# Attention with a relative bias, then a snake feed-forward layer, on one core: the loads of the prologue put in another order

## The chip, the cores and the metric

The kernel runs on one core of one Trainium2 chip. The metric is the device time of one execution in microseconds (us); every kernel is run several times, and the median is compared. The engines are named as in the profile: PE is TensorE, DVE is VectorE, ACT is ScalarE, POOL is GpSimd, and SP is SyncE, which here only issues DMAs. ACT and POOL issue DMAs too, each into a queue of its own.

## The reference

Two layers follow each other. The first is attention over 8 batches of 8 heads, with 576 positions of 64 elements, and a bias that depends only on the distance between two positions. The second takes the result as 4608 rows of 512 and is a feed-forward layer with a periodic activation.

```python
# attention: q, k, v are [8, 8, 576, 64], bias_table is [32, 8]
scores = scale * np.matmul(q, k.transpose(0, 1, 3, 2))
n = np.abs(pos[:, None] - pos[None, :])
bucket = np.where(n < 16, n, large)        # large: logarithmic in n, at most 31
scores = scores + bias_table[bucket].transpose(2, 0, 1)[None]
attn = softmax(scores)
x = (attn @ v).transpose(0, 2, 1, 3).reshape(4608, 512)
# feed-forward: w_in is [512, 2048], w_out is [2048, 512], alpha is [2048]
h = x @ w_in
g = h + np.sin(alpha * h) ** 2 / (alpha + 1e-9)
out = g @ w_out
```

Inputs and output are float32. The kernel works in float16 with float32 sums.

## The kernel before

**Steady work.** The kernel goes through the batches t = 0 to 7. For each it works on four pairs of heads. For a pair, PE multiplies q and k into PSUM (`sc`), ACT takes the exponential into a tile `u` (line 594; two such tiles take turns), DVE multiplies a band of `u` by a table of exponentiated biases (lines 606 and 623, tables `mhr` and `m2r`), and PE multiplies `u` by v (`av`). The last 64 of the 576 key positions don't fill a block of 128, so their v rows of two heads share a tile of their own, `vh`, beside the main tile `v`; every `av` product begins with the `vh` matmul. DVE divides by the row sums, PE turns the result round, and it is put into `xT`. After a batch's attention comes one block of 512 rows of the second layer: 16 steps f = 0 to 15, in each of which PE multiplies `xT` by `w_in` (four matmuls), ACT takes the sine (line 715), one of ACT, DVE and POOL squares it (lines 722 and 724; POOL only in block 0), and DVE forms g (line 729). The products of g with `w_out` (`mo`) are put between other work of PE, mostly into the next batch's attention.

**Prologue.** For batches 0 and 1, q and k come in by plain loads (tiles `natx`, `nat`) and PE turns them round (lines 495 and 501); from batch 2 on they are staged in DRAM by POOL's DMAs (`stage_kq`, line 330) and loaded with a transposing DMA. v of batches 0 and 1 is loaded as float32 into a staging area that lies inside the tile of `w_out` (`vst`, `vhst`), and POOL casts it into `v` and `vh` (`cast_v`, lines 367 and 369). The loads of `w_out` must therefore come behind the casts of v of batch 1. POOL also loads `w_in` and clears the second set of key tiles (`clear`, lines 391 to 399).

The bias table is made on the chip: a matmul with a constant `phi` gives a row of 512 values a head (`e_sb`, 8 partitions); ACT writes it to DRAM (`e_dram`), and `m2r` and `mhr` are read back from there with one element of offset per partition. POOL loads `m2r` of the first two heads, SP loads `mhr` and the rest of `m2r`. alpha is loaded by SP behind these, turned round on PE (line 541), and 1/alpha is made from it.

**Order.** Each engine runs its instructions in the order in which they are emitted. The prologue's order is written out by hand in the kernel's body (lines 429 to 472). All that follows is ordered by a planner (`Plan`): it knows a cost for each task and engine and times before which a task can't start (`T_M2` and `T_MH` for the bias tables, `T_V` for v, `T_TR1` for k and q of batch 1, `T_W` and `T_WO` for the weights; the second number is for the later pairs, q, or batch 1), and at each step it emits the task that can start first. These times are constants in the source; the chip waits on semaphores whatever they say. The planner counts POOL as free from its start time on; the prologue's work on POOL is not in it. The staging of batch 2 is emitted with the first matmul of batch 0, so on POOL it stands directly behind the prologue.

Of the kernel before, what the change touches and what calls it, by code (L numbers as in the profile page):

```python
# [10 lines left out]
F16 = mybir.dt.float16  # L11
F32 = mybir.dt.float32
# [38 lines left out]
class Cell:  # L51
    v = None
# [105 lines left out]
OFFSET = 8  # L158
T_START = 7.0
T_PAIR = ((7.0, 8.5), (10.5, 13.0), (10.5, 13.0))  # L160
T_M2 = (16.7, 20.5)
T_MH = (18.5, 20.5)
T_V = (17.7, 47.5)
T_TR1 = (37.5, 41.5)
T_W = 31.0
T_WO = 58.0
WARM0 = 6
WARM1 = 1
AV_PRI = 250
# [18 lines left out]
def kernel(  # L188
# [39 lines left out]
    for x in range(EW - 1):  # L228
# [18 lines left out]
    w_out16 = sgl.tile([128, NF, DM], F16, name="w_out16")  # L247

    wv = w_out16.rearrange("p f n -> p (f n)")
    vst = wv[:, 0 : 2 * 4 * H * D].bitcast(F32).rearrange("p (c h d) -> p c h d", c=4, h=H)  # L250
    vhst = wv[:, 2 * 4 * H * D : 2 * 4 * H * D + 2 * NP * D].bitcast(F32).rearrange(
        "p (hp d) -> p hp d", hp=NP
    )
# [103 lines left out]
    def load_v32(t, eng):  # L357
        vp = v[t].rearrange("h s d -> s h d")
        for c in range(4):
            eng.dma_start(out=vst[:, c], in_=vp[128 * c : 128 * c + 128])  # L360
        vq = v[t].rearrange("(hp two) s d -> two s hp d", two=2)
        for z in range(2):
            eng.dma_start(out=vhst[64 * z : 64 * z + 64], in_=vq[z, 512:S])  # L363

    def cast_v(t, engs):
        for c in range(4):
            engs[c].tensor_copy(out=vs[t][:, c, :, 0:D], in_=vst[:, c])
        for z in range(2):
            engs[4 + z].tensor_copy(  # L369
                out=vhs[t][64 * z : 64 * z + 64, :, VC * z : VC * z + D],  # L370
                in_=vhst[64 * z : 64 * z + 64],
            )

    def load_nat(dst, h0, h1, src, eng):

        eng.dma_start(out=dst, in_=src[h0:h1].rearrange("h (p i) d -> p h (i d)", i=SI))  # L376
# [32 lines left out]
    def cast0(kq, eng):  # L409
        eng.tensor_copy(  # L410
            out=natb[:, kq], in_=nat0[:, kq].rearrange("s two (i d) -> s i two d", i=SI)
        )

    def load_m2r(eng, h0, h1):

        eng.dma_start(
            out=m2r[:, h0:h1],
            in_=bass.AP(tensor=e_dram, offset=EW * h0, ap=[[1, 128], [EW, h1 - h0], [1, XW]]),
        )

    def load_mhr(eng):
        for z in range(2):
            eng.dma_start(
                out=mhr[64 * z : 64 * z + 64],
                in_=bass.AP(tensor=e_dram, offset=EW * z + 192,
                            ap=[[1, 64], [2 * EW, NP], [1, 192]]),
            )

    load_nat(nat0[:, 0], 0, 2, k[0], nc.sync)
    load_nat(nat0[:, 1], 0, 2, q[0], nc.sync)  # L430
    nc.scalar.dma_start(out=tabN, in_=bias_table)
    nc.scalar.dma_start(
        out=tabL,
        in_=bass.AP(tensor=bias_table.tensor, offset=bias_table.offset + (NB - 1) * H,
                    ap=[[0, NB], [1, H]]),
    )
    nc.scalar.dma_start(out=phi_sb, in_=phi_h.ap())
    nc.sync.dma_start(out=id_sb, in_=idm.ap())
    nc.scalar.preload_act_table_set(EXP_SET)
    for kq, src in ((0, k), (1, q)):  # L440
        load_nat(nat1[:, kq, 0:2], 2, 4, src[0], nc.gpsimd)
    load_v32(0, nc.sync)
    for kq, src in ((0, k), (1, q)):
        load_nat(nat1[:, kq, 2:6], 4, H, src[0], nc.gpsimd)

    nc.vector.memset(zz, 0.0)
    clear(nc.vector, 0)
# [5 lines left out]
    warm(WARM1)  # L453
    nc.scalar.activation(out=e_sb, in_=eps_[0:H, 0:EW], func=AF.Copy)
    nc.scalar.dma_start(out=e_dram.ap(), in_=e_sb)
    cast0(0, nc.vector)
    cast0(1, nc.gpsimd)
    load_m2r(nc.gpsimd, 0, 2)
    load_mhr(nc.sync)
    load_m2r(nc.sync, 2, H)  # L460
    nc.sync.dma_start(out=alphaN, in_=moe_alpha.rearrange("(f p) -> f p", p=128))
    nc.sync.dma_start(out=idf_sb, in_=idf.ap())
    P_ = nc.gpsimd
    load_w_in16((0,))
# [21 lines left out]
    def plan_tr(t, p, kq, pri, nb, deps=()):  # L486

        b, c = Buf("mo"), Cell()

        def mm(e):  # L490
            c.v = new_mo().bitcast(F16)
            for i in range(SI):
                x = i * SN
                if t == 0 and p == 0:
                    nc.tensor.transpose(
                        out=c.v[:, x : x + SN], in_=natb[:, kq, i], identity=id_sb[0:SN, 0:SN]
                    )
                    continue
                for z in range(2):
                    h = 2 * p - 2 + z if t == 0 else 2 * p + z  # L500
                    nc.tensor.transpose(
                        out=c.v[64 * z : 64 * z + 64, x : x + SN],
                        in_=(nat1 if t == 0 else nat2)[:, kq, h, D * i : D * i + D],
                        identity=id_sb[0:SN, 0:SN],
                    )

        def cp(e):
            pin = c.v[:, 0:S].rearrange("d (i p) -> d p i", i=SI)

# [24 lines left out]
        return [x], [plan.add({"DVE": 0.25}, tail, [x], pri + 30)]  # L534
# [322 lines left out]
```

## Time and profile before

| | |
|---|---|
| median of 6 runs | 423.59 us (421.27 to 425.47) |
| the profiled execution's own time | 423.19 us |
| its span in the profile | 421.4 us |
| granted PE clock, mean | 0.975 |
| busy: PE, ACT, DVE, POOL | 398.5, 335.8, 292.1, 89.2 us |
| DMA moved | 41.90 MB, 99 GB/s over the span |

The profile is of one execution. In its lists, a row has the start in us, the duration in us, the engine, the line of the kernel, the operation with what it writes and reads, and in brackets how long the engine was idle before and what ended that. A "q" behind an engine's name (SPq, POOLq) is its sequencer, which issues DMAs. A table of stretches has, for each, the busy time and the number of instructions of PE, weight loads, DVE, ACT and POOL, then the granted PE clock as a share of full speed, the busy share of the DMA engines and the GB/s that they moved. The chain is followed back from the last instruction, at each step to what released it.

The tile names in the trace are those of the memory: v's staging area appears as `w_out`, so `w_out<-in_v_dram` is a load of v and `w_out<-in_moe_w_out_dram` one of the weights.

### The profile page before, as it was taken

Reading aid. Unit: us, or ns where it says so; the run is one execution under the profiler, and the core shown is the slowest. Engines: PE = TensorE matmul, PEld = TensorE weight load, DVE = VectorE, ACT = ScalarE, POOL = GpSimd, SP = SyncE. Lnnn points to the kernel's source line nnn. Section 1 sums busy time; section 2 is a strip of 40 time slices with the busy share of each in tenths; the row PEclk is TensorE's granted clock in tenths of the full one; section 3 lists DMA queues with packets and bytes.
Section 4 is the critical chain, followed back from the end, with each engine's and each line's share of the span. In section 5 each row is a group of like instructions: output and inputs, shape, how many; then the busy total and the mean of one; then the engine's idle time right before and its main releaser. Section 6 shows DMA issues by size and latency. Waiting matters only on the chain.

```text
span 421.4 us, 8752 instructions
## 1 busy us (share of the span) xinstructions
PE 398.5 (95%) x3518; PEld 230.2 (55%) x3518; DVE 292.1 (69%) x683; ACT 335.8 (80%) x497; POOL 89.2 (21%) x100
## 2 busy tenths in 40 slices
PE   6786778999999999999999999999999999999996
PEld 2465334775467545764576456644775466544442
DVE  5868568675966695769666967687667867799300
ACT  4747648887988899879987998889888988899411
POOL 3376837206200350017000800040000000000000
PEclk8869979999999999999999999999999999999999
DMA  9989599998990399029920992095000010000111
GB/s 179 199 173 220 87 186 166 148 133 98 149 173 27 98 153 169 27 62 155 175 56 32 161 179 75 26 151 131 27 26 26 0 51 26 26 2 0 51 75 75
DMA packets 136232, 41.90 MB, mean 99 GB/s; under 512 B 121720, under 2 KB 130736, under 8 KB 136192
## 3 DMA queue, kind: packets, MB, share of 16 engines
q0 software_dynamic: 89632, 18.26, 52.1%
q1 hardware_dynamic: 46400, 23.05, 24.5%
q8 instruction: 27, 0.44, 0.4%
q14 instruction: 13, 0.11, 0.1%
q10 hardware_dynamic: 160, 0.04, 0.0%
HBM read 37.76 MB, written 16.52 MB: 129 GB/s over the span
## 4 chain that ended last, share of the span: by engine, by line
PE 85%; DMA 7%; POOL 4%; SPq 2%; DVE 1%; ACT 0%; issue 0%; POOLq 0%; ACTq 0%
PE sc L402 44%; PE mo L402 29%; PE av L402 10%; DMA w_out<-in_v_dram 6%; PE av L676 2%; SPq L360 1%; SPq L363 1%; DVE g L729 1%; POOL w_out L386 1%; POOL w_out L360 1%; DMA tabN<-in_bias_table_dram 1%; POOL staged_k L330 1%; POOL staged_q L330 1%; POOL w_in L381 0%; POOL nat L376 0%; ACT s L715 0%
## 5 line engine op out<-in xcount | busy, mean ns | idle before, releaser
L594 ACT ACTIVATE u<-sc 128x768 f16<-128x768 f32 (+1 forms) x224 | 165.7, 789 | 33.9 <-PE sc L402 29.6
L402 PE MATMUL mo<-w_out,g 128*128 128x512 f16 x576 | 156.3, 379 | 0.0
L402 PE MATMUL sc<-xT,w_in 128*128 128x512 f16 x576 | 132.9, 383 | 5.5 <-DVE g L729 5.5
L729 DVE SCALAR_TENSOR_TENSOR g<-sq,inv_a,sc 128x512 f16<-128x512 f16 x144 | 104.7, 747 | 13.5 <-ACT sq L722 6.1
L715 ACT ACTIVATE s<-sc,alphaT 128x512 f16<-128x512 f32 x144 | 92.3, 678 | 16.5 <-PE sc L402 15.7
L402 PEld LDWEIGHTS <-w_in 128*128 128x128 f16 x576 | 55.9, 98 | 71.6 <-issue 8.7
L402 PE MATMUL sc<-qT,kz 128*128 128x192 f16 (+1 forms) x512 | 90.8, 292 | 4.0 <-DVE g L729 1.5
L623 DVE TENSOR_TENSOR u<-u,m2r 128x512 f16<-128x512 f16 (+1 forms) x192 | 70.5, 388 | 20.0 <-ACT u L594 17.5
L402 PEld LDWEIGHTS <-g 128*128 128x128 f16 x576 | 55.7, 98 | 45.2
L402 PEld LDWEIGHTS <-u 128*128 128x128 f16 x1440 | 56.1, 98 | 12.6 <-issue 3.2
L402 PEld LDWEIGHTS <-kz 128*128 128x128 f16 x512 | 43.8, 99 | 24.7 <-issue 7.1
L348 POOL DMA_DIRECT2D v<-in_v_dram x24 | 21.3, 901 | 161.9 <-PE av L402 161.9
L402 PE MATMUL av<-v,u 128*128 128x65 f16 x1280 | 55.5, 195 | 0.0
L722 ACT ACTIVATE sq<-s 128x512 f16<-128x512 f16 x73 | 46.0, 630 | 2.3
L402 PE MATMUL av<-vh,u 128*128 128x130 f16 x160 | 35.5, 222 | 3.0 <-POOL vh L369 3.0
L665 DVE RECIPROCAL rd<-av 128x6 f32<-128x6 f32 x64 | 12.0, 187 | 37.2 <-PE av L402 37.2
L666 DVE TENSOR_TENSOR xn<-av,rd 128x384 f16<-128x384 f32 x64 | 31.4, 491 | 2.2
L724 DVE TENSOR_TENSOR sq<-s 128x512 f16<-128x512 f16 x66 | 28.4, 431 | 3.5 <-ACT s L715 2.9
L484 DVE COPY outs<-mo 128x512 f32<-128x512 f32 x27 | 18.6, 690 | 10.0 <-PE mo L402 9.9
L676 PEld LDWEIGHTS <-xn 128*128 128x128 f16 x160 | 13.9, 99 | 17.1 <-DVE xn L666 5.4
L482 ACT ACTIVATE outs<-mo 128x512 f32<-128x512 f32 x9 | 5.4, 597 | 22.4 <-PE mo L402 22.4
L676 PE MATMUL av<-id_sb,xn 128*128 128x128 f16 x160 | 19.5, 222 | 3.0 <-DVE xn L666 3.0
(66 smaller groups left out, 189.4 us busy)
## 6 DMA issues: line engine op xcount, KB each, us to landing
out_dram<-outs SPq DMA_DIRECT2D x36, 256.0 KB, 2.0
staged_k<-in_k_dram POOLq DMA_DIRECT2D x6, 576.0 KB, 11.7
staged_q<-in_q_dram POOLq DMA_DIRECT2D x6, 576.0 KB, 17.4
kz<-kraw SPq DMA_DIRECT2D x12, 288.0 KB, 6.8
v<-in_v_dram POOLq DMA_DIRECT2D x24, 128.0 KB, 5.8
w_in<-in_moe_w_in_dram POOLq DMA_DIRECT2D x4, 512.0 KB, 7.9
w_out<-in_moe_w_out_dram POOLq DMA_DIRECT2D x4, 512.0 KB, 9.3
w_out<-in_v_dram SPq DMA_DIRECT2D x4, 256.0 KB, 9.5
```

The costliest lines, as they stand in the source:

```text
L348: nc.gpsimd.dma_start(out=vs[t % 2][:, c, :, 0:D], in_=vp[128 * c : 128 * c + 128],)
L402: nc.tensor.matmul(out=out, lhsT=lhsT, rhs=rhs, start=start, stop=stop)
L484: k_of(e).tensor_copy(out=o, in_=i)
L594: nc.scalar.activation(out=o, in_=x, func=AF.Exp, scale=0.125)
L623: nc.vector.tensor_tensor(out=io, in0=io, in1=m2[:, 2 * p : 2 * p + 2, x0 : x0 + hi - lo], op=ALU.mult,)
L665: nc.vector.reciprocal(out=r, in_=a[:, :, :, D])
L666: nc.vector.tensor_tensor(out=xn.v[:, 0:nq].rearrange("p c (z d) -> p c z d", z=2), in0=a[:, :, :, 0:D], in1=r.unsqueeze(3).to_broadcast([ ...
L676: nc.tensor.transpose(out=tr.v[:, qc - q0 : qc - q0 + 128], in_=xn.v[:, i], identity=id_sb)
L715: nc.scalar.activation(out=s16.v, in_=h.v, func=AF.Sin, scale=alphaT[:, f : f + 1])
L722: nc.scalar.activation(out=sq.v, in_=s16.v, func=AF.Square)
L724: k_of(e).tensor_tensor(out=sq.v, in0=s16.v, in1=s16.v, op=ALU.mult)
L729: nc.vector.scalar_tensor_tensor(out=gcell[b].v[:, f, :], in0=sq.v, scalar=inv_a[:, f : f + 1], in1=h.v, op0=ALU.mult, op1=ALU.add,)
```

## The change

It has four parts. First, the table pieces of the first two heads (`m2r` of heads 0 and 1, `mhr` of pair 0) are copied on SP from `e_sb` in SBUF and no longer read from `e_dram`; for that the last main piece of v of batch 0 and its two `vh` pieces go behind them on SP, and the pieces of the other heads are loaded by POOL. Second, alpha and its identity matrix are loaded by ACT at the start, and `phi` goes first there. Third, v of batch 1 is staged in a tile of its own (`v1st`), so that the four `w_out` loads are issued directly behind its loads, ahead of its casts, and the clearing of the second key tiles moves on POOL to before the table loads. Fourth, the planner's times change, and one of its costs.

```diff
-T_M2 = (16.7, 20.5)
-T_MH = (18.5, 20.5)
-T_V = (17.7, 47.5)
-T_TR1 = (37.5, 41.5)
-T_W = 31.0
-T_WO = 58.0
+T_M2 = (12.0, 17.0)
+T_MH = (12.5, 17.0)
+T_V = (18.0, 45.0)
+T_TR1 = (33.5, 37.5)
+T_W = 30.0
+T_WO = 54.0
...
+    v1st = sgl.tile([128, 2 * (4 * H + NP) * D], F16, name="v1st")
+    vst, vhst = [], []
+    for x in (wv, v1st):
...
+    def near(eng):
+        for h in range(2):
+            eng.dma_start(
+                out=m2r[:, h],
+                in_=bass.AP(tensor=e_sb.tensor, offset=e_sb.offset + EW * h,
+                            ap=[[EW, 1], [1, 128], [1, XW]]),
+            )
+        for h in range(2):
+            eng.dma_start(
+                out=mhr[64 * h : 64 * h + 64, 0],
+                in_=bass.AP(tensor=e_sb.tensor, offset=e_sb.offset + EW * h + 192,
+                            ap=[[EW, 1], [1, 64], [1, 192]]),
+            )
...
     def load_mhr(eng):
         for z in range(2):
             eng.dma_start(
-                out=mhr[64 * z : 64 * z + 64],
-                in_=bass.AP(tensor=e_dram, offset=EW * z + 192,
-                            ap=[[1, 64], [2 * EW, NP], [1, 192]]),
+                out=mhr[64 * z : 64 * z + 64, 1:NP],
+                in_=bass.AP(tensor=e_dram, offset=EW * (z + 2) + 192,
+                            ap=[[1, 64], [2 * EW, NP - 1], [1, 192]]),
             )
...
+    nc.scalar.dma_start(out=phi_sb, in_=phi_h.ap())
     nc.scalar.dma_start(out=tabN, in_=bias_table)
     nc.scalar.dma_start(out=tabL, ...)
-    nc.scalar.dma_start(out=phi_sb, in_=phi_h.ap())
+    nc.scalar.dma_start(out=alphaN, in_=moe_alpha.rearrange("(f p) -> f p", p=128))
+    nc.scalar.dma_start(out=idf_sb, in_=idf.ap())
     nc.sync.dma_start(out=id_sb, in_=idm.ap())
...
-    load_v32(0, nc.sync)
+    vp = v[0].rearrange("h s d -> s h d")
+    for c in range(3):
+        nc.sync.dma_start(out=vst[0][:, c], in_=vp[128 * c : 128 * c + 128])
...
     nc.scalar.dma_start(out=e_dram.ap(), in_=e_sb)
+    near(nc.sync)
+    nc.sync.dma_start(out=vst[0][:, 3], in_=vp[384:512])
+    vq = v[0].rearrange("(hp two) s d -> two s hp d", two=2)
+    for z in range(2):
+        nc.sync.dma_start(out=vhst[0][64 * z : 64 * z + 64], in_=vq[z, 512:S])
     cast0(0, nc.vector)
-    cast0(1, nc.gpsimd)
-    load_m2r(nc.gpsimd, 0, 2)
-    load_mhr(nc.sync)
-    load_m2r(nc.sync, 2, H)
-    nc.sync.dma_start(out=alphaN, in_=moe_alpha.rearrange("(f p) -> f p", p=128))
-    nc.sync.dma_start(out=idf_sb, in_=idf.ap())
-    P_ = nc.gpsimd
+    cast0(1, P_)
+    clear(P_, 1)
+    load_mhr(P_)
+    load_m2r(P_, 2, H)
     load_w_in16((0,))
-    cast_v(0, (P_, P_, P_, P_, P_, P_))
+    cast_v(0, P_, range(6))
     load_w_in16((1, 2, 3))
     for kq, src in ((0, k), (1, q)):
-        load_nat(nat2[:, kq], 0, H, src[1], nc.gpsimd)
-    load_v32(1, nc.gpsimd)
-    clear(nc.gpsimd, 1)
-    cast_v(1, (P_, P_, P_, P_, P_, P_))
+        load_nat(nat2[:, kq], 0, H, src[1], P_)
+    load_v32(1, P_)
     load_w_out16()
+    cast_v(1, P_, range(6))
...
-        m = plan.add({"PE": 0.4 if t == 0 and p == 0 else 0.7}, mm, deps, pri, nb, new=[b])
+        m = plan.add({"PE": 0.4 if t == 0 and p == 0 else 0.5}, mm, deps, pri, nb, new=[b])
```

More of the change, by code (lines that the diff above doesn't have):

```diff
@@ L249 @@
     wv = w_out16.rearrange("p f n -> p (f n)")
[L250 to L253, printed above, removed]
+    v1st = sgl.tile([128, 2 * (4 * H + NP) * D], F16, name="v1st")
+    vst, vhst = [], []
+    for x in (wv, v1st):
+        n4 = 2 * 4 * H * D
+        vst.append(x[:, 0:n4].bitcast(F32).rearrange("p (c h d) -> p c h d", c=4, h=H))
+        vhst.append(
+            x[:, n4 : n4 + 2 * NP * D].bitcast(F32).rearrange("p (hp d) -> p hp d", hp=NP)
+        )
     zz = sgl.tile([128, 512], F16, name="zz")
@@ L359, in load_v32, with cast_v @@
         for c in range(4):
-            eng.dma_start(out=vst[:, c], in_=vp[128 * c : 128 * c + 128])
+            eng.dma_start(out=vst[t][:, c], in_=vp[128 * c : 128 * c + 128])
         vq = v[t].rearrange("(hp two) s d -> two s hp d", two=2)
         for z in range(2):
[L363 to L369, printed above, removed]
+            eng.dma_start(out=vhst[t][64 * z : 64 * z + 64], in_=vq[z, 512:S])
+    def cast_v(t, eng, cs):
+        for c in cs:
+            if c < 4:
+                eng.tensor_copy(out=vs[t][:, c, :, 0:D], in_=vst[t][:, c])
+                continue
+            z = c - 4
+            eng.tensor_copy(
                 out=vhs[t][64 * z : 64 * z + 64, :, VC * z : VC * z + D],
-                in_=vhst[64 * z : 64 * z + 64],
+                in_=vhst[t][64 * z : 64 * z + 64],
             )
@@ L412, in cast0 @@
         )
+    def near(eng):
[10 more added lines that the diff above has]
+                            ap=[[EW, 1], [1, 64], [1, 192]]),
+            )
     def load_m2r(eng, h0, h1):
@@ L423, in load_mhr @@
             eng.dma_start(
-                out=mhr[64 * z : 64 * z + 64],
-                in_=bass.AP(tensor=e_dram, offset=EW * z + 192,
-                            ap=[[1, 64], [2 * EW, NP], [1, 192]]),
+                out=mhr[64 * z : 64 * z + 64, 1:NP],
+                in_=bass.AP(tensor=e_dram, offset=EW * (z + 2) + 192,
+                            ap=[[1, 64], [2 * EW, NP - 1], [1, 192]]),
             )
+    P_ = nc.gpsimd
     load_nat(nat0[:, 0], 0, 2, k[0], nc.sync)
     load_nat(nat0[:, 1], 0, 2, q[0], nc.sync)
+    nc.scalar.dma_start(out=phi_sb, in_=phi_h.ap())
     nc.scalar.dma_start(out=tabN, in_=bias_table)
@@ L440 @@
     for kq, src in ((0, k), (1, q)):
-        load_nat(nat1[:, kq, 0:2], 2, 4, src[0], nc.gpsimd)
-    load_v32(0, nc.sync)
+        load_nat(nat1[:, kq, 0:2], 2, 4, src[0], P_)
+    vp = v[0].rearrange("h s d -> s h d")
+    for c in range(3):
+        nc.sync.dma_start(out=vst[0][:, c], in_=vp[128 * c : 128 * c + 128])
     for kq, src in ((0, k), (1, q)):
-        load_nat(nat1[:, kq, 2:6], 4, H, src[0], nc.gpsimd)
+        load_nat(nat1[:, kq, 2:6], 4, H, src[0], P_)
     nc.vector.memset(zz, 0.0)
```

## The prediction

> **What bounds the kernel now.** I read the page first. PE is busy 398.5 of 421.4 us, and section 2 shows where the other 22.9 us are: in the first seven slices and in the last.
>
> ```profile
> PE 398.5 (95%) x3518; PEld 230.2 (55%) x3518; DVE 292.1 (69%) x683; ACT 335.8 (80%) x497; POOL 89.2 (21%) x100
> PE   6786778999999999999999999999999999999996
> DMA  9989599998990399029920992095000010000111
> ```
>
> The table by stretches of 5 us puts 18.9 us of PE's idle time before 75 us; from 80 to 187 us PE is busy in every microsecond (20.00, 43.00 and 44.00 us of as many). The work behind the prologue is thus a fixed block on a full engine: whatever the prologue gives or takes, the end gives or takes. Next, the chain that ended last, for 0 to 60 us alone:
>
> ```profile
> 0.74 2.59 DMA tabN<-in_bias_table_dram
> 3.33 0.04 issue
> 3.37 2.77 SPq L360
> ...
> 12.83 8.93 DMA w_out<-in_v_dram
> ...
> 21.89 0.40 POOL vh L369
> ...
> 22.35 1.59 POOL w_in L381 x3
> 23.95 1.57 POOL nat L376 x2
> 25.51 2.60 POOL w_out L360 x3
> 28.12 16.13 DMA w_out<-in_v_dram
> ...
> 45.72 2.94 POOL w_out L386 x4
> 48.66 2.23 POOL staged_k L330
> 50.89 2.23 POOL staged_q L330
> ...
> 53.25 1.04 POOL sq L724
> ...
> 54.32 0.76 DVE g L729
> ...
> 55.12 5.03 PE sc L402 x14
> ```
>
> The chain is not PE's, it is POOL's queue. The tail rows of v of batch 0 (called vh0 here) land at 21.76; POOL casts them, issues w_in, k and q of batch 1 and v of batch 1 (28.12), whose last big piece lands at 44.25; it casts these, then issues four w_out loads (2.94), staged_k and staged_q of batch 2, and only then squares the sine that block 0 of the second half has wanted since 47.7 (end of the third sine in the timeline). DVE waits 4.64 us for that square, PE 4.71. The windows show what follows: PE empty from 52 to 54, and a granted clock of 0.5 until after 58.
>
> ```profile
> 52.00:54.00 2.00, 0.00 (x0) 0.00 (x0) 0.00 (x0) 0.00 (x0) 1.87 (x2) 0.51 1.19 195
> 54.00:56.00 2.00, 0.88 (x3) 0.32 (x3) 1.68 (x3) 0.00 (x0) 1.07 (x2) 0.50 1.24 206
> 56.00:58.00 2.00, 2.00 (x6) 0.67 (x5) 1.30 (x3) 0.69 (x1) 0.25 (x1) 0.50 1.24 206
> ```
>
> So the change is priced at one point: when POOL reaches that first square.
>
> **w_out ahead of the casts of v of batch 1.** This takes 2.94 us of issue from between the last cast (ends 45.7) and staged_k. The issues move to behind 34.2, where POOL has time: it spends 34.24 to 40.33 on the memsets of clear(1), which move away, and the first cast began at 40.70. They don't go out at once. POOL's DMAs show a rotation of eight: the two vh issues of batch 1, the 16th and 17th on the queue, waited 1.49 and 2.40 us for w_in loads, the 8th and 9th. With two more POOL DMAs in front (three table loads for one), the four w_out loads follow the landings of k of batch 1 (23.92 + 12.4 = 36.3), of q (24.70 + 15.0 = 39.7) and of the first two v pieces (by 40.7 and 41.9, when their casts began). The last is out at 41.9 + 0.8 = 42.7; six casts behind it (4 x 0.62 + 2 x 0.43 = 3.3) end at 46.0, against 45.7 before. Net 2.94 - 0.3 = 2.6 us earlier. That w_out itself lands earlier than 47.88 + 12.0 = 59.9 brings nothing: its first matmul ran at 69.3. The tile of its own for v of batch 1 adds no instruction; v of batch 0 stays under w_out, and its casts are done 14 us before the first w_out issue.
>
> **clear(1) moved to 6.4 us.** POOL waited 5.45 us there for e_dram (until 11.88); the memsets take 6.1 (34.24 to 40.33), so the cover falls short by 0.65. A DVE instruction of 16 columns lasted 1.75 us and ended at 36.28, beside a POOL memset that ended at 36.30; in the new place the kt copy at 8.46 can be held the same way until 10.6, but DVE was idle from 8.84 to 10.30. Cost 0 to 0.3 on DVE; the 0.65 goes into the next part.
>
> **POOL's new table loads.** Two far mhr loads and the far m2r load stand where one m2r load stood: about 0.65 + 0.65 (the vh issues' row) + 0.72, against 0.72. w_in's first load thus goes at 12.59 + 0.65 + 1.3 = 14.5, the casts of v of batch 0 run from 15.1 to 17.6. Hidden as long as vh0 lands later than that (18.8 and 21.8 before).
>
> **When vh0 lands** is the one large unknown, since the chain hangs on it one for one (each POOL step behind it is issue time or a full DMA queue: 9 tenths busy from 25 to 42). Later: (a) the near tables, 2 x 96 + 2 x 24 = 240 KB, go out on SP in front of the last v piece and vh0. At the stage's 179 to 199 GB/s that is 1.3 us; at the slowest row for such a table (m2r, 192 KB, 5.8 us from issue to landing) it is 7.3. (b) The SP and ACT queues show the same rotation of eight: the third v load, ninth of the two queues together, started at 3.37, just behind the landing of tabN, the first. With alpha and identf in front, already the first v load is ninth and waits for the first landings (k of batch 0 at 0.74 + 3.4 = 4.1) where it went at 2.17. DMA is 9 tenths busy with other loads then, so 0 to 2.0, I take 0. (c) The far tables, 720 KB, came behind vh0 on SP and now go beside it on POOL: 0 to 720/190 = 3.8. Earlier: (d) 192 KB of m2r leave POOL: 1.0. (e) w_in's first 512 KB are issued 1.9 us later and behind the far tables; vh0's two 64 KB loads took 9.7 and 8.9 us beside it, so up to about 3.5 can come back. I let (c) and (e) cancel, and (a) at the stage's rate and (d) nearly do: 0, with ends of -3.5 and +7.
>
> SP waits in front of the near tables until e_sb is there (6.69); behind it in line are the last v piece and vh0. Their issue was held anyway (the last v piece until 9.05, vh0 until 12.79), so this wait costs 0.
>
> [...]
>
> **Gone covers.** The near tables land some 3 to 9 us earlier (DVE waited 2.88 for mhr at 22.66), but the first av matmul waited for vh0's cast at 22.29, not for a table: nothing. With pair 1's tables there by then, too, the attention of batch 0 may end 0 to 4 us earlier than 43.8. That only lengthens the wait for POOL's square: nothing. **alpha** on ACT: its transpose at 26.45 waited for no DMA; its 2.67 + 0.57 us of issue leave SP, where nothing is queued behind them until 63.6; on ACT the phi load gets out 0.93 earlier, the table set goes in 0.9 later and still ends before the exp, which follows DVE's memsets at 5.1 as before: 0.
>
> **The planner's new times** and the 0.5 for 0.7 reorder the prologue. I can't read the order from a profile; one step of the second half (four matmuls, 0.86 us) done before or behind the stall is the unit: plus or minus 1.
>
> **Sum.** The square at 53.25 - 2.6 = 50.65, PE again at 52.5 instead of 55.1, the profiled execution 423.19 - 2.6 = 420.6. The median of the runs is 0.4 above the profiled one: 421.0. The stall shrinks from 4.7 to 2.1 us unless the attention ends earlier. Of the half-clock time behind it (55.1 to about 58.6) up to 1.75 us could then come back; I take none, since the clock was already down (0.63 from 20 to 25) behind the idle stretch of 3.02 us that ended at 22.34, and an earlier attention lengthens this one. [...]
>
> **Rivals.** (1) vh0 comes 2 to 3.5 us earlier, because w_in no longer crosses it: 421.0 less 2 to 3.5, 417.5 to 419. For: 64 KB took over 9 us. Against: 720 KB of far tables take w_in's place. (2) It comes 1 to 4 us later and eats the gain: 422 to 425. For: 240 + 720 - 192 = 768 KB more can be ahead of it. (3) Slower: the near tables, read out of one partition each, hold the SP queue; vh0 comes 7.3 - 1.0 = 6.3 later, 421.0 + 6.3 = 427.3. It decides from the point where vh0 lands 2.6 us later, at 24.4; SP's issue of vh0 would then lie behind 15 us. (4) The change doesn't do what it says: w_out does not load right behind v, as the rotation holds its issues to 36 to 42 us. True in part, but the gain comes from the place in POOL's line, not from the bytes: only if the rotation held the fourth issue beyond 44 would it cost, 1 us or so.
>
> **Numbers.** Measurement of this kernel can tell about 0.5%, 2.1 us, from no change. Forecast case (vh0 within 1.5 us of before, 419.5 to 422.5): 0.40. Rival 1: 0.13. Rival 2: 0.25. Rival 3: 0.20. Rival 4: 0.02. Faster by over 0.5% (below 421.5): 0.33 of the first and all of rival 1: 0.46. Slower (above 425.7): rival 3 and a tail of rival 2: 0.24. The rest, 0.30, is no change. Range: from 416.5 (rival 1 and the planner's 1 us) to 427.5 (rival 3 at the row's price).
>
> **What would show it.** Right: staged_k on POOL directly behind the vh casts, at about 46; the first square near 50.7; DVE's wait for it near 2 us, or longer with an earlier start of the second half; no wait for mhr near 22. Wrong: vh0's cast behind 24.4, SP's near issues lasting microseconds, or v of batch 1 landing later than 46. A PE wait for something else between 50 and 75 us would break the step from the stall to the end.

## The result, and the profile after

The changed kernel takes 427.17 us (median of 18 runs, 424.38 to 431.54); the kernel before, run beside it, 423.03 (39 runs). The ratio is 1.0088, with a 95% interval of 1.0064 to 1.0112: slower, by some 3.7 us by the ratio. The profiled execution took 425.41 us, before it was 423.19. The ratios here and below are of undisturbed executions alone (experiments 3 and 7 leave out four runs each, experiment 4 eight of twelve) and need not be the quotients of the medians beside them.

The page of the changed kernel, with the same three lines as were shown of before:

```profile
PE 399.5 (94%) x3518; PEld 230.3 (54%) x3518; DVE 292.3 (69%) x684; ACT 335.4 (79%) x495; POOL 91.8 (22%) x103
PE   5559799999999999999999999999999999999996
DMA  9869999999990299119930997095100010000111
```

The difference still lies in the first seven slices of PE, but it has moved to the front: the first three fell from 6, 7 and 8 to 5 each, the fourth, sixth and seventh rose to 9. The chain of the changed kernel, from 12 us on, says why (start, duration, engine or transfer, line):

```profile
12.95 1.25 SPq L428
14.25 4.46 SPq L428
18.75 9.79 DMA w_out<-in_v_dram
28.60 0.69 POOL v L372
...
30.54 2.55 PE av L408 x45
...
53.08 5.49 PE sc L408 x17
```

It goes through SP's queue. L428 is the copying of `mhr` from `e_sb`; the last main piece of v of batch 0 gets out behind it at 18.75 and lands at 28.54, vh0 at 29.54 (before: 21.76). The casts end at 30.5, the first av matmul follows at once. But after that the chain goes to and fro between PE and DVE, up to the second half, which starts at 53.08: POOL's square isn't on it any more. SP's part of the timeline, and the table by stretches (busy time of PE, weight loads, DVE, ACT, POOL, then clock, DMA share, GB/s):

```profile
8.47 4.44 SPq L422 DMA_DIRECT2D m2r<-e_sb  x2
12.95 5.75 SPq L428 DMA_DIRECT2D mhr<-e_sb  x2
18.75 1.57 SPq L482 DMA_DIRECT2D w_out<-in_v_dram  x1
20.36 4.31 SPq L485 DMA_DIRECT2D w_out<-in_v_dram  x2
```

```profile
15.00:20.00 5.00, 2.13 (x21) 1.54 (x20) 0.00 (x0) 2.30 (x4) 2.99 (x5) 1.00 0.75 28
20.00:25.00 5.00, 1.16 (x14) 0.54 (x14) 2.19 (x5) 0.30 (x1) 0.00 (x0) 1.00 0.90 214
```

From 15 to 20 us the DMA engines were busy for 0.75 of the time and moved 28 GB/s. Before, the same stretch was:

```profile
15.00:20.00 5.00, 3.48 (x39) 1.85 (x37) 4.65 (x10) 4.89 (x7) 1.08 (x2) 1.00 1.04 190
```

The packets in the changed kernel's trace are those of the near tables: from 14 to 20 us 32 to 37 of 768 bytes start in each microsecond, about 360 ns long, 26 KB/us in all (rates here count 1000 bytes as a KB; by 1024 it is 25.4). Those of the two `m2r` pieces ran from 12.9 to 20.7. POOL had issued the far tables from 13.60 to 15.7, and the first of their packets ran at 19.9: what is slow also stands in front of the others. `m2r` of the first two heads landed at 17.64 and 21.44 (before: 17.66), `mhr` of pair 0 at 23.27 and 25.69.

Who waited for that, in the timelines of DVE, PE and POOL (in brackets the idle time ahead and what ended it):

```profile
21.56 1.43 DVE L649 TENSOR_TENSOR u<-u,m2r 128x512 f16<-128x512 f16 x4 [7.62 <-DMA m2r<-e_sb]
23.02 0.76 DVE L510 COPY qT<-mo 128x576 f16<-128x576 f16 x1
23.84 0.82 PE L408 MATMUL sc<-qT,kz 128*128 128x384 f16 x2 [6.71 <-DVE qT L510]
53.90 2.20 POOL L334 DMA_DIRECT2D staged_k<-in_k_dram  x1
58.46 1.31 POOL L750 TENSOR_TENSOR sq<-s 128x512 f16<-128x512 f16 x1
```

DVE stood 7.62 us at the first multiply by `m2r`. Behind it in line was the copy of q of pair 1 (23.02), which needs no table at all, and PE stood 6.71 us for that copy. POOL came to staged_k at 53.90 and to its first square at 58.46, 5.2 us later than before (53.25); but no one waited for it, since the attention of batch 0 was as late. So the end moved by 2.2 us in this execution (421.4 to 423.6 of span) and not by 5.2: PE's idle time grew from 22.9 to 24.1, its busy time from 398.5 to 399.5.

The clock column says 1.00 up to 50 us here, and it can't be taken at its word. The same group of two `sc` matmuls took 0.82 us at 23.84 and 0.49 at 34.35, and a group of eight `av` 0.65 at 30.60 and 0.40 at 34.73 (0.65 is also what it took before, at 22.95, where the clock's record gave 0.50). In this trace the record begins only at 32.55; until then PE ran at the pace of a granted 0.5, and so the means of the clock (0.975 before, 0.996 after) aren't compared below:

```profile
30.60 0.65 PE L408 MATMUL av<-v,u 128*128 128x65 f16 x8
34.73 0.40 PE L408 MATMUL av<-v,u 128*128 128x65 f16 x8
```

### The profile page after: what moved, and what is told of

Same layout as the page of the kernel before. It is cut to its first block, busy times and chain, and to the rows that moved or that the text cites. A ratio compares the mean times of both kernels' runs of the same rounds, so it can differ in the third digit from the quotient of the medians.

```text
span 423.6 us, 8757 instructions
## 1 busy us (share of the span) xinstructions
PE 399.5 (94%) x3518; PEld 230.3 (54%) x3518; DVE 292.3 (69%) x684; ACT 335.4 (79%) x495; POOL 91.8 (22%) x103
## 4 chain that ended last, share of the span: by engine, by line
PE 87%; DVE 5%; DMA 3%; SPq 2%; ACT 1%; POOL 0%; issue 0%; ACTq 0%; DVEq 0%
PE sc L408 44%; PE mo L408 29%; PE av L408 11%; DMA w_out<-in_v_dram 2%; PE av L702 2%; SPq L428 1%; DMA tabL<-in_bias_table_dram 1%; DVE g L755 1%; DVE xn L692 1%; DVE kz L510 1%; DVE u L649 1%; DVE kt L556 1%; DVE qT L510 1%; ACT u L620 1%; DVE natx L416 0%
## 5 line engine op out<-in xcount | busy, mean ns | idle before, releaser
L620 ACT ACTIVATE u<-sc 128x768 f16<-128x768 f32 (+1 forms) x224 | 166.2, 789 | 39.9 <-PE sc L408 34.1
L691 DVE RECIPROCAL rd<-av 128x6 f32<-128x6 f32 x64 | 12.0, 188 | 37.7 <-PE av L408 37.7
L750 DVE TENSOR_TENSOR sq<-s 128x512 f16<-128x512 f16 x65 | 28.3, 435 | 5.1 <-ACT s L741 4.7
L702 PE MATMUL av<-id_sb,xn 128*128 128x128 f16 x160 | 19.4, 219 | 1.6 <-DVE xn L692 1.4
## 6 DMA issues: line engine op xcount, KB each, us to landing
staged_q<-in_q_dram POOLq DMA_DIRECT2D x6, 576.0 KB, 17.7
```

Of the source, the lines that this page charges most:

```text
L620: nc.scalar.activation(out=o, in_=x, func=AF.Exp, scale=0.125)
L691: nc.vector.reciprocal(out=r, in_=a[:, :, :, D])
L702: nc.tensor.transpose(out=tr.v[:, qc - q0 : qc - q0 + 128], in_=xn.v[:, i], identity=id_sb)
L750: k_of(e).tensor_tensor(out=sq.v, in0=s16.v, in1=s16.v, op=ALU.mult)
```

## Experiments

The theory from this profile: the near copies, each out of one partition, run at some 26 KB/us and hold SP's queue and the DMA engines (the prediction's third rival). Rivals: their place ahead of vh0 alone does it; or parts that were priced at nothing cost something.

**1. The same tables from DRAM, at the same place on SP** (e1_near_dram: the change with)

```diff
-    ap=[[EW, 1], [1, 128], [1, XW]]   # source e_sb
+    ap=[[1, 128], [1, XW]]            # source e_dram; mhr alike
```

> The changed kernel with one edit: the four near table loads read from e_dram and no longer from e_sb; place, sizes and queue stay. Theory (one source partition): in the changed kernel they moved 25 KB/us from 13.5 to 21.4 us and held every DMA queue; from DRAM rows of the same size should move at 200 KB/us, vh0 lands at 19 to 22 instead of 29.5, v of batch 1 at 42 to 45 instead of 53.0, staged_k goes out at 43 to 46, and the time is 418 to 421.5, 2 to 5 us under the kernel before. Rival (place on SP): four loads and their wait in front of the last v piece and vh0 delay these whatever they read; vh0 lands at 27 to 30 and the time stays at 425 to 428.

424.79 us, ratio 1.0048 [1.0014, 1.0082]. The near tables landed between 16.7 and 18.3, as fast as the theory says; vh0 still landed at 27.13, where the theory had 19 to 22 and the rival 27 to 30, and staged_k came at 51.76. By the ratios a little under half of the loss went (the two intervals overlap; experiment 6 has a like result), so both are partly right: the slow source, and the place. vh0 was issued at 16.49 and 17.21, 4 to 5 us earlier than in the change; its packets then ran beside POOL's far tables and w_in's first piece, which landed at 24.86.

**2. The near copies alone** (e2_near_only, on the kernel before)

```diff
     nc.scalar.dma_start(out=e_dram.ap(), in_=e_sb)
+    near(nc.sync); <last v piece, vh0>      # mhr of pairs 1 to 3 and the far m2r stay on SP
-    load_m2r(nc.gpsimd, 0, 2)
```

> The kernel before with the near tables alone: read from e_sb on SP in front of the last v piece and vh0; w_out, alpha, the clearing and the planner's times as before. Theory (one source partition): vh0 lands 7 to 9 us later than 21.8; the chain through POOL still has the four w_out issues in it, so the first square on POOL comes 7 to 8 us later than 53.3 and the time is 428 to 431. Rival (the planner's new times or the other moves did the harm): vh0 within 3 us of before and the time 423 to 425.

426.53 us, 1.0067 [1.0037, 1.0096]. The part alone costs 2.8 us. The price by vh0 missed: it landed at 24.70, 2.9 later and not 7 to 9. w_in's first piece had landed at 15.89, before vh0 was issued, and POOL issued no load from 6.94 to 25.47, so nothing competed. Here POOL's line was last, as the prediction has it:

```profile
57.06 1.03 POOL L744 TENSOR_TENSOR sq<-s 128x512 f16<-128x512 f16 x1
58.93 7.31 PE L402 MATMUL sc<-xT,w_in 128*128 128x512 f16 x24 [7.19 <-DVE g L749]
```

**3. w_out alone** (e3_wout_only, on the kernel before, with `v1st`)

```diff
     clear(nc.gpsimd, 1)
+    load_w_out16()
     cast_v(1, (P_, P_, P_, P_, P_, P_))
-    load_w_out16()
```

> The kernel before with only v of batch 1 in a tile of its own and the four w_out loads issued behind the clearing and ahead of its casts. The prediction's step: the first square on POOL 2.6 us earlier (50.7), PE's stall in block 0 2.1 us instead of 4.7, time 420 to 421.5 (2.6 less, 0.6%). Rival: POOL's line is not what binds, or w_out's bytes get in the way of v of batch 1: within 1 us of before.

422.59 us, 0.9946 [0.9912, 0.9979]: 2.3 us gained by the ratio, where the prediction had 2.6. The traced execution (423.73, no faster than before) doesn't show the step, though. vh0 landed at 16.13 and staged_k came at 44.28, but PE waited for alpha's identity matrix, which landed at 33.42 behind the far `m2r`, and then the square waited for its sine and not the reverse:

```profile
33.55 0.26 PE L545 MATMUL mo<-idf_sb,alphaN 16*128 16x16 f32 x1 [7.27 <-DMA idf_sb<-identf]
55.10 1.03 POOL L728 TENSOR_TENSOR sq<-s 128x512 f16<-128x512 f16 x1 [6.39 <-ACT s L719]
```

**4. Before without POOL's squares** (e4_no_pool_sq)

```diff
-            if b == 0:
-                engs["POOL"] = 1.2
```

> The kernel before with POOL taken from the engines that may square the sine in block 0; DVE and ACT take all. If the chain through POOL's line is what the prologue costs, the 4.7 us stall of PE and the half-clock stretch behind it go: 3 to 6 us less, 417.5 to 420.5, less some 1 us of added work on DVE and ACT (five squares of 0.4 to 0.6). If attention of batch 0 or the w_out load binds right behind, under 1 us less.

Its runs took from 416.6 to 429.2 us, with a gap from 418.4 to 422.8; the median is 424.65, the ratio 0.9881 [0.9832, 0.993]. In the traced execution (423.79) PE's longest wait in block 0 is 2.08 us and no longer 4.71, and the time is no shorter. So whether the square was the bound of before stays open.

**5. Everything but the near copies, and the near copies behind vh0** (e5_all_but_near, e6_near_behind)

```diff
 # e5: tables and v of batch 0 as before
-    near(nc.sync)                  # and the last v piece, vh0 behind it
-    load_mhr(P_); load_m2r(P_, 2, H)
+    load_m2r(P_, 0, 2); load_mhr(nc.sync); load_m2r(nc.sync, 2, H)
 # e6
-    near(nc.sync); <last v piece, vh0>
+    <last v piece, vh0>; near(nc.sync)
```

> The changed kernel with its tables and the tail of v of batch 0 as before: vh0 ahead of every table on SP, m2r of the first two heads on POOL from DRAM, mhr and the rest of m2r on SP. The own tile for v of batch 1, w_out ahead of the casts, clear at 6 us, alpha at the start on ACT and the planner's new times stay. Theory (the copies out of e_sb and what had to go behind them are the whole loss): vh0 lands near 22 again, staged_k starts near 46, time near 421, the forecast. Rival (the parts that were priced at nothing, alpha in front of tabL, clear beside DVE's cast, the planner's times, cost 1 to 2 us of their own): vh0 near 22 to 23, first qk product near 9.5 to 10 instead of 8, time 423 to 424.5, above the kernel that moves w_out alone (422.6).

430.82 us, 1.0166 [1.0116, 1.0216]: slower than the change itself, though vh0 landed at 16.04 and staged_k came at 45.12, both earlier than forecast. This fells the idea that all hangs on POOL's chain. Two waits of this kernel (total, times, longest), DVE's row and POOL's row:

```profile
DVE u L629 <- DMA m2r<-e_dram: 14.0, 2, 9.3
PE av L682 <- DVE xn L672: 12.8, 3, 8.2
33.37 1.23 DVE L629 TENSOR_TENSOR u<-u,m2r 128x512 f16<-128x512 f16 x3 [9.34 <-DMA m2r<-e_dram]
45.12 2.20 POOL L334 DMA_DIRECT2D staged_k<-in_k_dram  x1
```

The far `m2r`, issued by SP at 14.42, landed at 33.28 (before: 24.12). With vh0 there at 16, POOL issues w_in, k, q and v of batch 1 from 17.7 on, and SP's load starves beside them. Before, POOL stood until 21.8 waiting for vh0; that wait was what let the far tables through. Kernels e3, e8, e11 and e12 show the same pair: vh0 at 15.9 to 17.5, far `m2r` at 32.2 to 33.7. In e4 and e7 both lie between: vh0 at 19.4 and 19.1, far `m2r` at 27.0 and 26.9. None of these six is as slow as e5. The late table costs most with the new times, which put its multiply early: moving it to POOL ahead of w_in gives 8.7 us there (e5 to e14, by the medians) and 1.6 with the old times (e8 to e10).

> The changed kernel with the four copies out of e_sb issued behind the last main piece and vh0 on SP. Theory (the copies hold whatever is queued behind them, and the DMA engines that serve them, while they run at about 25 KB a microsecond): vh0 lands before 18, its casts wait for POOL's table loads and w_in instead; the near tables land 3 to 8 us later than in the change (m2r near 24, mhr near 27), so PE waits for the bias of pair 0 until 25 to 27; the chain through POOL is free of vh0, staged_k at 47 to 49, time 423 to 425. Rival (only the order on SP counts, the copies themselves harm nothing but what is behind them): time near 421.

428.1 us, 1.0102 [1.0047, 1.0157]: missed. vh0 landed at 15.98, as the theory had it, and staged_k came at 49.86, a little behind its 47 to 49, but the near tables, last in line, landed at 19.2 to 28.3, and the attention itself was late:

```profile
24.25 1.43 DVE L649 TENSOR_TENSOR u<-u,m2r 128x512 f16<-128x512 f16 x4 [9.83 <-DMA m2r<-e_sb]
```

So the copies cost wherever they stand: in front they delay vh0, behind they delay themselves.

**6. The source spread over four partitions** (e13_near_spread)

```diff
     nc.scalar.activation(out=e_sb[0:H], in_=eps_[0:H, 0:EW], func=AF.Copy)
+    for r in range(1, 4):          # rows of heads 0 and 1, shifted by 32 r
+        nc.scalar.activation(out=e_sb[32 * r : 32 * r + 2, 0 : EW - 32 * r],
+                             in_=eps_[0:2, 32 * r : EW], func=AF.Copy)
-    ap=[[EW, 1], [1, 128], [1, XW]]
+    ap=[[32 * EW, 4], [1, 32], [1, XW]]
```

> The changed kernel with the rows that the near copies read laid out on four partitions 32 apart: ACT copies the rows of heads 0 and 1 three more times from PSUM, shifted by 32, 64 and 96 elements, so that row p of a table is read from partition 32*(p/32). Issue places and bytes stay as in the change; ACT has three more copies (its e_sb copy's row, some 0.5 us each). Theory (the source's partitions set the rate): the 240 KB need 2.4 us at four times the 25.4 KB a microsecond of the change, or 4.9 us at twice; m2r near has landed by 17 to 18, vh0 by 22 to 25, staged_k at 48 to 50, time 422 to 425. Rival (the rate goes by the size and the kind of packet, 768 B from SBUF to SBUF, not by the partitions): near again at 21 to 26, time 427. [...]

425.95 us, 1.0051 [1.0027, 1.0075]. (`mhr`'s 64 rows lie on two of the four partitions.) Size and kind of packet are the same, the rate is not: in the fastest microsecond, 14 to 15 us, 63 KB/us of near packets against 26, and POOL's far tables flow from 14 on; the `m2r` pieces took 4.6 us (13.0 to 17.6) and not 7.8. The same stretch of the table by stretches shows it:

```profile
15.00:20.00 5.00, 2.84 (x23) 1.65 (x21) 1.60 (x5) 3.25 (x5) 2.69 (x5) 1.00 0.87 200
```

The one partition was the brake. Yet vh0 landed at 26.90: it is issued on SP behind the copies, at 18.41 and 22.54 (the issue at 18.41 alone lasts 4.1 us; why, the trace doesn't show), and its packets meet 720 KB of far tables and w_in's first piece on POOL's queue, which landed at 25.00. Taking the brake away gives 1.6 us of the 3.7; its place and what is around it keep the rest.

**7. The planner's times and the small parts alone** (each on the kernel before)

```diff
 # e7_times_only: the six T_ constants of the change, and
-    {"PE": 0.4 if t == 0 and p == 0 else 0.7}
+    {"PE": 0.4 if t == 0 and p == 0 else 0.5}
 # e11_alpha_act: ACT issues phi, tabN, tabL, alphaN, idf_sb in this order
-    nc.sync.dma_start(out=alphaN, ...); nc.sync.dma_start(out=idf_sb, ...)
 # e12_clear_early
     cast0(1, nc.gpsimd)
+    clear(nc.gpsimd, 1)
```

> The kernel before with the change's planner times and its cost of 0.5, and nothing else. Forecast of the prediction: within 1 us of before, either way (422 to 424). Rival (the earlier times pull work of the second half and of batch 1 in front of work that could have run, and cost the place on PE): 425 to 427, with a PE wait in the first 75 us that before doesn't have.

> The kernel before with phi first on ACT and alpha and its identity matrix behind tabL on ACT, and nothing else. The prediction's price: 0. Theory (tabL becomes third instead of second, lands 1.0 to 1.5 us later, and the chain over e_sb to the tables starts that much later; against it, alpha no longer queues behind the far tables): tabL lands at 5.5 to 6.5, e_sb at 7.7 to 8.2, no PE wait for alpha; 422.5 to 425. Rival (alpha at the start is a gain, as late alpha costs PE up to 7 us in single executions): 421 to 422.

> The kernel before with the memsets of clear(1) moved to about 6 us, in front of the near m2r load on POOL, and nothing else. The prediction's price: 0.65 on POOL's table load, 0 to 0.3 on DVE. Theory (DVE's SBUF-to-SBUF copies wait for the end of POOL's memset, as the cast of 0.60 us that took 1.63 in the changed kernel): DVE's first cast and kt copies lose 1 to 2 us in all between 6 and 13 us, time 0 to 1.5 us above before, 423 to 424.5. Rival (free): 422.5 to 423.5, or below, since DVE's copies beside 34 to 40 us become faster.

Times: 426.09 us, 1.0037 [1.0002, 1.0072], 1.6 us slower by the ratio, as the rival had it; in its profile DVE waits 5.22 us for `m2r` and PE 4.5 for the copy of q queued behind. alpha: 1.0 [0.9981, 1.0019]. tabL landed at 6.32, and `e_sb` was written out 1.4 later than before (8.10 against 6.71), with nothing to show for it in the time. clear: 1.0013 [0.9989, 1.0038]; no difference. In these two traces vh0 landed some 5.5 us earlier than before (15.86 and 16.28), and the time is the same. PE stood elsewhere, in the clear kernel 6.44 us for alpha, and the first square waited for its sine (3.23 and 4.38 us). So an earlier vh0 alone, the prediction's first rival, gains nothing here.

**8. The old times in the changed kernel** (e9_after_old_times)

> The changed kernel with the planner times and the cost of before (m2r from 16.7 instead of 12.0, and so on). Theory (the new times put pair 0's bias multiply on DVE ahead of the next pairs' copies, and PE pays for it while m2r is late): DVE copies q and k of pair 1 before it multiplies by m2r, PE's wait of 6.7 us for qT shrinks to under 2; 424.5 to 426. Rival (POOL's first square at 58 us binds as soon as the attention is earlier, so the gain turns into a wait for it): PE gets the work done earlier, but DVE then waits 3 to 5 us for POOL's square and the time stays at 426.5 to 428.

428.38 us, 1.0128 [1.0103, 1.0152]: the theory missed, the rival's time was nearer, though DVE has no long wait for POOL's square. In this kernel the new times are the better ones, by 0.4%. With the copies of pairs 1 and 2 ahead of the multiply, PE has that work done early and then stands in one piece until vh0's cast. The second half starts earlier, too, and there two DVE copies are held beside POOL's staging. Rows of PE, DVE and PE:

```profile
30.12 0.27 PE L408 MATMUL av<-vh,u 128*128 128x130 f16 x1 [8.40 <-POOL vh L375]
53.94 4.30 DVE L556 COPY kt<-kz 64x64 f16<-64x64 f16 x2
59.07 1.86 PE L408 MATMUL sc<-xT,w_in 128*128 128x512 f16 x4 [3.97 <-DVE g L755]
```

With vh0 late, another order only moves the stalls. What the times are worth shows where the loads are in order, as in the next kernels.

**9. Towards a kernel whose loads are in order** 

```diff
 # e8_wout_alpha: e3, and on SP behind vh0
+    alphaN, idf_sb
     load_mhr(nc.sync); load_m2r(nc.sync, 2, H)
-    alphaN, idf_sb
 # e10_far_pool: e8, and
-    load_m2r(nc.sync, 2, H)
     load_m2r(nc.gpsimd, 0, 2)
+    load_m2r(nc.gpsimd, 2, H)             # w_in comes behind it
 # e15_far_pool_times: e10 with the T_ constants and the 0.5 of the change
```

> The kernel that moves w_out alone (422.6), with alpha and its identity matrix issued on SP in front of mhr and the far m2r, still behind vh0. Theory (alpha's landing behind the far tables cost PE 7 us in one profiled execution there, and in before it was at times late too): idf lands before 25, no PE wait for it; time 420.5 to 422.5. Rival (that late landing was one execution's, and where alpha is late another wait behind it ends as late): 422.6 as without it. Price: two issues, some 1.3 us of SP, put mhr that much later.

> The kernel with w_out and alpha moved (421.5) and the far m2r pieces issued by POOL behind the near ones and ahead of w_in, instead of by SP at 15.8. Theory (with vh0 early, POOL's w_in, k, q and v of batch 1 are issued from 18 us on and starve the SP queue's far m2r until 32, where DVE waited 6.4 us and PE 5.0; ahead of w_in on the same queue they land before 24): no such wait, time 418.5 to 420.5. Rival (the starved bytes only change places: w_in and with it k and q of batch 1 and w_out come later, POOL's first square too): 421 to 422.

> The fastest kernel so far (419.9: w_out, alpha and the far m2r moved) with the change's planner times and its cost of 0.5. Theory (times that are earlier than the landings put DVE's bias multiply ahead of the copies that PE needs; m2r near lands at 17 there, the times say 12): DVE waits 3 to 5 us for m2r near, PE 3 to 5 for qT, time 421 to 423. Rival (in the changed kernel the old times were slower, 428.4 against 427.2, so the new ones are the better order as soon as the loads are right): 418.5 to 420.

e8: 421.5 us, 0.995 [0.9919, 0.998], no wait for alpha, 5.0 us of PE's waiting for the far `m2r` (32.17). e10: 419.88, 0.9924 [0.9899, 0.9948]; the far `m2r` lands at 19.18 and that wait is gone. e15: 426.57, 1.0044 [1.0008, 1.008]: the new times alone cost 1.2% there, 5.1 us by the ratios, more than the theory's 421 to 423 has it. DVE's rows:

```profile
17.33 1.63 DVE L627 TENSOR_TENSOR u<-u,m2r 128x512 f16<-128x512 f16 x4 [4.46 <-DMA m2r<-e_dram]
18.99 0.76 DVE L488 COPY qT<-mo 128x576 f16<-128x576 f16 x1
26.41 0.26 DVE L610 TENSOR_TENSOR u<-u,mhr 128x192 f16<-128x192 f16 x1 [6.66 <-DMA mhr<-e_dram]
```

The times say 12.0 and 12.5 for tables that landed at 17.24 and 26.33; in between, copies that PE needs stand behind the multiplies. (In e10 both `mhr` pieces had landed by 23.20, so part of this is a later landing.)

**10. The change without its copies, with the far tables first** 

```diff
 # e14_rest_far_pool: e5, and
-    load_m2r(nc.sync, 2, H)
     load_m2r(P_, 0, 2)
+    load_m2r(P_, 2, H)
 # e16_rest_far_old: e14 with the T_ constants and the 0.7 of before
```

> The changed kernel with no copies out of e_sb (430.8) and its far m2r pieces issued by POOL behind the near ones and ahead of w_in, instead of by SP at 14.4. Theory (there the far m2r, starved beside w_in until 33.3, held DVE 9.3 us with the whole attention behind it): no wait for m2r beyond 25, vh0 at 17 to 22, staged_k at 45 to 47, time 419.5 to 422.5, so that all parts but the copies give what was forecast. Rival (the planner's times, alpha's place and the early clear cost by themselves): 423 to 426, with DVE still held by m2r of pair 0 in front of PE's copies.

> The changed kernel with no copies out of e_sb, the far m2r on POOL ahead of w_in (422.2), and now with the planner times and the cost of before. Theory (the new times cost wherever the tables land later than they say: 1.6 us alone, 6.7 on the kernel of 419.9): DVE's multiply by m2r of pair 0 comes behind the copies of pairs 1 and 2, PE's wait of 2.9 us for qT at 20 goes, time 418.5 to 421. Rival (here mhr lands at 18, early enough for the new times, and the earlier end of the attention puts DVE's kt copies beside POOL's staging, where they take 4 us): 422 to 424.

e14: 422.16 us, 0.9964 [0.994, 0.9987]. e16: 419.14, 0.9894 [0.9861, 0.9926]. Both theories held in the time. Going from before to the change over these two: the loads in the new order without near copies give 1.06% (4.5 us), the planner's times take back 0.70% (3.0 us), and the near copies, with vh0 behind them and the far `mhr` on POOL, take 1.24% (5.2 us). The three add up to the 0.88% measured by their making. The split holds for this order of steps alone: with the near copies in, the new times gain (e9), without them they cost.

**11. What is left at the start of the second half** 

```diff
 # e17_kt_act: e16, and
-    nc.vector.tensor_copy(out=kts[t][r, p, r], ...)
+    copy_on("ACT" if t else "DVE", kts[t][r, p, r], ...)
 # e18_kt_act_nosq: e17, and
-    engs["POOL"] = 1.2
```

In e16 staged_k comes at 43.84, and this stands beside it, in the timelines of DVE, POOL and PE:

```profile
44.16 4.29 DVE L536 COPY kt<-kz 64x64 f16<-64x64 f16 x2
45.54 2.72 POOL L334 DMA_DIRECT2D staged_q<-in_q_dram  x1
49.29 1.62 PE L408 MATMUL sc<-xT,w_in 128*128 128x512 f16 x4 [3.97 <-DVE g L735]
```

> The fastest kernel (419.1) with the kt copies of batch 1, SBUF to SBUF, on ACT instead of DVE. In three profiled executions two such copies of DVE took 4.2 to 4.3 us, where 0.36 is usual, because POOL was issuing staged_k and staged_q, and ended with them; PE then waited 3.97 us for g. Theory (DVE's copy is held until POOL's issue ends, and that is the rest of the stall): DVE busy normally at 44 to 48; but POOL's square at 48.4 comes next in line for the same block, so the stall only shrinks to the 2 to 3 us before it; 418 to 419.5. Rival (nothing but the label of the stall changes, POOL's square binds at the same time): 419.1, and DVE idle 4 us for POOL's square where it was busy with kt.

> As the run before, and POOL squares nothing: ACT and DVE take its squares. Theory (with both, no engine that PE needs waits for POOL's staging): no PE wait of over 1.5 us between 44 and 52, the stall's 4 us and the half-clock stretch behind it come back; against that some 5 us of squares more on ACT and DVE in block 0, which are not full there; 415.5 to 418. Rival (the planner's order changes for the worse, or the work behind it meets w_out or batch 2 that has not landed): 418.5 to 421.

e17: 418.26 us, 0.987 [0.9839, 0.99], no clear step from e16 in time, but PE's 3.97 us wait is gone. e18: 415.5, 0.9807 [0.9764, 0.9849]: 1.9% faster than before, the fastest here. PE has no wait of over 1.5 us between 44 and 52 in it; the stretch that held 1.03 us of PE's work in e16 (first row) holds 4.95 (second row; in e17 it was 5.00, at a granted clock of 0.67):

```profile
45.00:50.00 5.00, 1.03 (x5) 0.38 (x4) 4.95 (x6) 0.69 (x1) 4.29 (x3) 0.96 1.24 206
45.00:50.00 5.00, 4.95 (x34) 2.29 (x33) 4.81 (x10) 4.75 (x9) 5.00 (x6) 1.00 1.30 203
```

## Why the prediction was wrong

**The step that failed** is the landing of vh0, which "When vh0 lands" puts at 0, no later than before. It landed at 29.54, 7.8 later, and two of its terms are mis-sized. Term (a) prices the 240 KB of near tables at the stage's 179 to 199 GB/s, 1.3 us. The `m2r` pieces alone, 192 KB, took 7.8 us, at 26 KB/us. e2 has this term by itself: vh0 2.9 later. The other is "(c) and (e) cancel". In e1, where the near tables were there by 18.3, vh0 still came 5.4 later than before, for it came behind w_in's first piece, and that behind the far tables. So it is in every trace in which w_in was on its way when vh0 was issued: 21.27 and 21.76 before, 24.86 and 27.13 in e1, 25.00 and 26.90 in e13, 27.67 and 29.54 in the change.

The prediction named both a bound from a row (7.3) and the reason to fear it, and chose the rate of rows that don't read out of single partitions. No row of the trace covered that source, which was a reason to set its third rival at least even.

**Luck.** That rival has the mechanism (near issues lasting microseconds on SP, vh0 behind 24.4), and its 427.3 stands beside 427.17 measured, but the number fits by two errors that cancel. vh0 came 7.8 later and not 6.3, and so did the square, 5.2 behind before, which is 7.8 less the 2.6 for w_out. By the prediction's one-for-one step the profiled execution would then be 5.2 slower; it was 2.2.

The rates that stand against term (a): out of one partition a table, 26 KB/us (25 over the 7.8 us of the `m2r` pieces); out of the four partitions of e13, 63 in the fastest microsecond and 43 over the 4.6 us of the same pieces, beside POOL's loads. More source partitions went with a higher rate; no run here measures the spread copies by themselves.

**A second step failed, unseen in the sum:** "one point", POOL's first square, on which the rest hangs one for one. It holds where POOL is last, as in e2. In e5 POOL reached staged_k at 45.12, better than the forecast's 46, and the time was 430.8. In e11 and e12 vh0 came some 5.5 us earlier and nothing was gained. Three other things were close behind and took over: the loads on SP's queue (far `m2r`, alpha) that starve once POOL is no longer held by vh0, which no term of the prediction covers; DVE's line, in which a multiply that waits for a table holds copies that PE needs ("gone covers: nothing"); and copies held beside POOL's staging. "Where a stall goes, what is late next" was asked only of POOL.

**The planner's new times** were given 1 us either way. They cost 1.6 us alone, 3.0 between e16 and e14, and 5.1 between e10 and e15, and gained 1.7 in the changed kernel itself (e9). The prediction took the near tables to land 3 to 9 us earlier; where they land later than the constants say (12.0 against 17.64 in the change), what is emitted behind them on DVE waits.

**Right, as far as it can be told:** w_out ahead of the casts, 2.6 us by the sum and 2.3 by e3's ratio, though e3's trace shows the gain on POOL's line (staged_k 4.3 earlier, vh0 being earlier too) and not at the square, so the agreement may be chance. The rotation: in e14 the four issues stood at 34.1, 37.7, 38.8 and 39.8, each behind a landing, and the casts ended at 43.8. alpha's place and the early clear: nothing in the time, by e11 and e12 (in the change, a cast on DVE took 1.63 us beside clear's memset, where 0.60 was usual; the interval of e12 would hide no more than 1.6). The step "a stall of 2.1 remains at POOL's square" was never reached in the change. That nothing of the half-clock time behind such a stall was counted back has a row for it: before, the record of the clock falls to 0.5 at 21.34, when PE had been idle for 2.0 us.

## What to carry to other kernels

Before pricing a transfer at the stage's rate, ask how many partitions it reads from; here a small table out of one partition, at 26 KB/us, held its own queue for 8 us and another queue's packets for 6. When a step is freed that held an engine, list what that engine will now issue and which loads it will crowd out: here the wait for vh0 was what let the tables through. Times given to a planner are promises about landings: a table promised too early puts a waiting instruction in front of work that needs no table.

## What the runs showed of the hardware

- Copies out of one source partition each ran at 26 KB/us, spread over four at up to 63; and while the slow copies ran, the packets of another queue, issued at 13.6 to 15.7, stood until 19.9.
- DVE's copies from SBUF to SBUF were held while POOL issued staged_k and staged_q: two `kt` copies took 4.23, 4.30 and 4.29 us in e5, e9 and e16, where 0.36 is usual, and ended within 0.2 us of that issue's end (49.55 against 49.54, 58.24 against 58.05, 48.45 against 48.26). A tensor_scalar took 3.01 in e15 (0.17 in e5 and e9) and ended at 47.85, the issue at 47.84. A tensor_tensor in SBUF (`sq<-s`) beside the same issue kept its 0.43 (the changed kernel, at 54.42).
- The granted clock in the rows can stand at 1.00 where its record has not begun (until 32.55 in the changed kernel) while PE runs slower (0.82 against 0.49 for the same two matmuls): a duration of one shape, early and late, is the safer sign.
- Which is issued first, w_in's first piece or vh0, went with some 6 us of vh0's landing in the clearest two executions: behind it (12.83 against 12.59, before) at 21.76, ahead of it (12.53 against 13.73, e11) at 15.86. Where POOL's table load came at about the same time as vh0 (e4, e7, e8), it was 17.4 to 19.4.
